# Loads and scores of an attention front end put into another order: third tile's q before the first regroupings, second tile's scores before the first mixing, k and v pieces spread over the double steps

## The chip, the cores and the metric

The program runs on one core of one Trainium2 chip. The metric is the device time of one execution in microseconds (us), as the median of several runs.

## The reference

Attention over 4 batches of 12 heads, 448 positions and 64 dimensions, whose heads are mixed by a 12 by 12 matrix before the softmax and by another one after it. Its output goes through an MLP-mixer block (a token MLP and a channel MLP, each with a residual).

```python
scores = (1 / np.sqrt(64)) * np.matmul(q, k.transpose(0, 1, 3, 2))
scores = np.einsum('bhij,hg->bgij', scores, w_pre)
scores = scores - np.max(scores, axis=-1, keepdims=True)
attn = np.exp(scores)
attn = attn / (np.sum(attn, axis=-1, keepdims=True) + 1e-09)
attn = np.einsum('bhij,hg->bgij', attn, w_post)
x = np.matmul(attn, v)                      # then (B, S, 768)
h = np.maximum(x.transpose(0, 2, 1) @ w_tok1, 0.0) @ w_tok2
u = x + h.transpose(0, 2, 1)
out = u + np.maximum(u @ w_ch1, 0.0) @ w_ch2
```

## The kernel before

**Tiles and groups.** The 448 query rows of a batch are four tiles `T` of 120, 120, 120 and 88 rows (`IT`), 16 tiles in all. `qk` computes the scores of one pair of heads of a tile on TensorE (8 matmuls in the trace) and copies them from PSUM into the tile `s` in SBUF, on ScalarE or, with `dve=True`, on VectorE. To mix heads by a matmul, the 12 heads of a query row must lie on partitions, so `regroup` (line 164) moves every 12th row of `s`, with all its heads, into a tile `r`: a DMA of 120 rows of 448 floats, SBUF to SBUF, on the queue of SyncE (SP). There are eight `r` tiles, so a regrouping is issued some eight groups ahead of its use. Two groups make a step.

**A step.** `pre` mixes the heads on TensorE (line 172, waits for two `r` tiles), `mx` takes the row maximum on VectorE, `ex` the exponential on ScalarE, `rec` the reciprocal on VectorE and the multiplication on GpSimd (POOL), `post` the second mixing on TensorE (line 214), `turn` transposes on VectorE. When a tile is complete, `av` multiplies by `v` in three pieces, and `store` writes the result `x` to DRAM.

**The order.** The main loop runs over double steps `J` from -2 on, two steps each, and the order of the calls in it is written out. Three tables say what a double step gets beside its steps: `score[J]` the `qk` calls for later tiles, `value[J]` the `av` calls, `loads[J]` the DMAs that bring q, k and v from DRAM. `loads[J + 1]` is issued at the end of double step `J`, behind that step's four regroupings. All these DMAs, regroupings, loads and stores alike, stand in one queue on SP, in program order; only a few of the first loads are issued by ScalarE. SP issues a DMA when its own waits are over, and each one waits too for the landing of the eighth DMA before it.

**Ahead of the loop** stand the loads of the first q and k, q of the second tile and a quarter of v, nine warm-up matmuls, the `qk` calls of tile 0, the first eight regroupings, and four of the six `qk` calls of tile 1; the other two stand in double steps -2 and -1.

**Behind the loop** come the transposes of `x` and the two MLPs, with weights that are split into two parts while TensorE works.

Of the kernel before, what the change touches and what calls it, by code (L numbers as in the profile page):

```python
# [19 lines left out]
B, H, S, D = 4, 12, 448, 64  # L20
DM = H * D
DT, DC = 256, 1536
JT = 4
IT = [(0, 120), (120, 120), (240, 120), (360, 88)]
GR = 10
HP = H // 2
# [10 lines left out]
def attn_mixer_kernel(  # L37
# [12 lines left out]
    nc = tc.nc  # L50
# [34 lines left out]
    AT, V = {}, {}  # L85
# [15 lines left out]
    NT = len(first)  # L101
# [9 lines left out]
    def load_q(T, h, m, eng):  # L111
        b, t = divmod(T, 4)
        i0, n = IT[t]
        if T not in Q:
            Q[T] = early.tile([128, HP, 120], F32, tag="q", bufs=3, name="q")
            if n < QP[t]:
                nc.gpsimd.memset(Q[T][:, :, n:QP[t]], 0.0)
        for s in range(2):
            o = H * i0 + (HP * s + h) * n
            eng[s].dma_start(  # L120
                out=Q[T][64 * s:64 * s + 64, h:h + m, :n],
                in_=q[b, :, o:o + m * n].rearrange("p (h i) -> p h i", h=m),
            )

    def load_v(b, part):
        if b not in V:
            V[b] = late.tile([128, H, JT, D], F32, tag="v", bufs=2, name="v")
        hs = slice(3 * part, 3 * part + 3)
        if part < 2:
            nc.sync.dma_start(out=V[b][:, hs], in_=v[b, :, hs])  # L130
            return
        lower, upper = slice(0, 64), slice(64, 128)
        nc.sync.dma_start(out=V[b][upper, hs, :3], in_=v[b, lower, hs, :3])
        nc.sync.dma_start(out=V[b][lower, hs, :3], in_=v[b, upper, hs, :3])
        nc.sync.dma_start(out=V[b][upper, hs, 3], in_=v[b, upper, hs, 3])

    def pair(tag, name):
        return (ps if tag == "pre" else ps_w).tile([128, 2, 512], F32, tag=tag, bufs=2, name=name)

    def qk(T, h, home="w", dve=False):  # L140
        b, t = divmod(T, 4)
        n = IT[t][1]
        if T not in S_t:
            S_t[T] = early.tile([120, H, S], F32, tag="s", name="s")
        p = pair(home, "qk")
        for c in (0, 64):
            m = min(64, QP[t] - c)
            for s in range(2):
                r = slice(64 * s, 64 * s + 64)
                nc.tensor.matmul(  # L150
                    out=p[c:c + m, s, :S], lhsT=Q[T][r, h, c:c + m], rhs=K[b][r, h, :], start=True, stop=True
                )
        if dve:
            nc.vector.tensor_copy(out=S_t[T][:n, h::HP, :], in_=p[:n, :, :S])
        else:
            nc.scalar.copy(out=S_t[T][:n, h::HP, :], in_=p[:n, :, :S])  # L156
# [111 lines left out]
    one = (nc.sync, nc.sync)  # L268
# [13 lines left out]
    for r in rt:  # L282
        nc.gpsimd.memset(r[:4], 0.0)
    load_q(1, 0, HP, one)
    load_v(0, 0)
    wz = et[0][:, 0].bitcast(BF16)
    nc.vector.memset(et[0], 0.0)
    for i in range(WARM):
# [4 lines left out]
    for x in range(2):  # L293
        ps_ = slice(64 * x, 64 * x + 64)
        nc.vector.tensor_tensor(
            out=kpre[ps_, :60].rearrange("p (i g) -> p i g", i=5),
# [5 lines left out]
    for s in range(2):  # L302
        ps_ = slice(64 * s, 64 * s + 64)
        for hf in range(2):
            nc.gpsimd.tensor_tensor(
                out=kpost[ps_, 32 * hf:32 * hf + 30].rearrange("p (g i) -> p g i", g=6),
# [165 lines left out]
    sf = [f // 2 for f in first]  # L472
    sl = [(f - 1) // 2 for f in first[1:]]
    loads = {J: [] for J in range(-2, ND)}
    score = {J: [] for J in range(-2, ND)}
    value = {J: [] for J in range(-2, ND)}
    for T in range(NT - 1):
        J = (sl[T] + 1) // 2
        n = sf[T + 2] // 2 - J
        if sf[T + 2] % 2 and sf[T + 2] // 2 > (sf[NT - 1] - 8) // 2:  # L480
            n += 1
        n = min(3, n)
        for hp in range(3):
            value[J + min(hp, n - 1)].append((T, hp))
    for h in range(HP):
        if h < 4:
            qk(1, h, ("pre", "w")[h % 2], h % 2 == 0)
        else:
            score[h - 6].append((1, h))
    for T in range(2, NT):  # L490
        hi = (sf[T] - 8) // 2
        lo = max((sl[T - 2] - 8) // 2 + 1 + (T == 4), hi - 2)
# [7 lines left out]
    uses = {}  # L500
    for J in range(-2, ND):
        score[J].sort()
        for T, h in score[J]:
            uses.setdefault((T, h), J)
    for T in range(2, NT):
        loads[max(-2, uses[T, 0] - 2)].append((load_q, T, 0, HP, one))
    for J, part in ((-1, 2), (0, 1), (2, 3)):
        loads[J].append((load_v, 0, part))
    for b in range(1, B):
        for h in range(0, HP, 2):  # L510
            J = uses[4 * b, 0] - 5 + h // 2
            loads[uses[4 * b, h] - 2 if b == 1 else J].append((load_k, b, h, 2, one))
        for part in range(JT):
            loads[sf[4 * b + 1] // 2 - 6 + part].append((load_v, b, part))

    def step(i):
        return steps[i] if 0 <= i < NS else []
# [284 lines left out]
```

## Time and profile before

| | |
|---|---|
| Median of 3 runs | 749.4 us (748.48 to 750.58) |
| Profiled execution, its own time | 757.26 us |
| Its span, from first to last instruction | 755.5 us |
| TensorE busy in the span | 735.6 us (97%) |
| VectorE, ScalarE, GpSimd busy | 410.7, 328.4, 303.7 us |
| Attention part, mixing steps | about 16 to 316 us |
| DMA: bytes, mean rate | 105.27 MB, 139 GB/s |
| TensorE clock granted | 1.0 in all slices |

The profiled execution is one run of the program with the profiler on; its 1.8 us outside of the span lie ahead of the first and behind the last instruction. An engine counts as busy while an instruction of it runs, matmuls by modelled ends. Idle time of an engine that nobody waits for costs nothing.

### The profile page before, as it was taken

The page shows a single profiled execution, that of the slowest core. Times are in us where ns is not written, and L with a number is a line of the kernel's source. Part 1 is how long each engine was busy: PE and PEld are TensorE (multiplying, and loading weights), DVE is VectorE, ACT ScalarE, POOL GpSimd, SP SyncE. Part 2 cuts the span into 40 slices and gives each one's busy share as a digit, 9 for nine tenths or more (in the row PEclk, how much of TensorE's full clock was granted, in tenths as well). Part 3 has the DMA queues.
Part 4 walks back from the last instruction along what each step waited for, and adds up shares of the span by engine and source line. Part 5 has one row for each costly group of instructions (what it writes and reads, how often), then busy time and mean ns, then how long its engine had stood idle before and what let it go on. Part 6 is the DMA issues. An engine that isn't in the chain of part 4 may idle for free. (4 is left out here: it accounts for less than half of the span.)

```text
span 755.5 us, 21850 instructions
## 1 busy us (share of the span) xinstructions
PE 735.6 (97%) x9209; PEld 570.5 (76%) x9209; DVE 410.7 (54%) x746; ACT 328.4 (43%) x732; POOL 303.7 (40%) x253
## 2 busy tenths in 40 slices
PE   8898999999999999899999999999999999999997
PEld 3354565556556555589988999999999999999997
DVE  3775676666766877778999999520004000220002
ACT  3776766776777777455544444300002000200000
POOL 3564665566656677757778777000000000000000
PEclk9999999999999999999999999999999999999999
DMA  6787667567756644735757655340003000020002
GB/s 180 240 232 213 199 194 229 190 192 217 231 175 228 217 165 159 265 104 198 252 178 221 169 170 162 147 146 1 1 1 146 1 1 1 0 74 1 0 1 74
DMA packets 66754, 105.27 MB, mean 139 GB/s; under 512 B 22835, under 2 KB 54624, under 8 KB 66144
## 3 DMA queue, kind: packets, MB, share of 16 engines
q1 hardware_dynamic: 66080, 102.96, 42.9%
q8 instruction: 73, 1.20, 0.7%
q10 hardware_dynamic: 480, 0.87, 0.5%
q14 instruction: 25, 0.20, 0.1%
q0 software_dynamic: 96, 0.03, 0.0%
HBM read 48.79 MB, written 16.52 MB: 86 GB/s over the span
## 5 line engine op out<-in xcount | busy, mean ns | idle before, releaser
L203 POOL TENSOR_TENSOR e<-e,sm 128x896 f32<-128x896 f32 x90 | 149.5, 1680 | 71.1 <-ACT e L189 25.9
L629 DVE SCALAR_TENSOR_TENSOR rl<-pc,rh 128x448 fp32r<-128x448 f32 x48 | 29.8, 621 | 218.7 <-ACT rh L628 218.7
L229 DVE STREAM_TRANSPOSE at<-post 128x896 f32<-128x896 f32 (+1 forms) x98 | 99.6, 1026 | 74.5 <-PE post L214 74.4
L628 ACT ACTIVATE rh<-pc 128x448 fp32r<-128x448 f32 x48 | 26.0, 542 | 232.9 <-PE pc L634 232.9
L189 ACT ACTIVATE e<-pre,sm 128x448 f32<-128x448 f32 x180 | 113.0, 640 | 5.5 <-DVE sm L198 4.8
L156 ACT COPY s<-qk 120x896 f32<-120x896 f32 (+1 forms) x91 | 81.6, 906 | 74.2 <-PE qk L150 70.5
L632 PE MATMUL pc<-u,w 128*128 128x448 f32 x288 | 105.3, 366 | 0.9 <-DVE u L665 0.9
L634 PE MATMUL pc<-u,w 128*128 128x448 f32 x288 | 105.2, 365 | 0.0
L633 PE MATMUL pc<-u,w 128*128 128x448 f32 x288 | 105.2, 365 | 0.0
L633 PE MATMUL po<-rl,w 128*128 128x448 f32 x288 | 105.2, 365 | 0.0
L634 PE MATMUL po<-rh,w 128*128 128x448 f32 x288 | 105.2, 365 | 0.0
L632 PE MATMUL po<-rh,w 128*128 128x448 f32 x288 | 105.2, 365 | 0.0
L180 DVE TENSOR_REDUCE sm<-pre 128x2 f32<-128x896 f32 x90 | 94.7, 1076 | 12.2 <-PE pre L172 12.1
L172 PE MATMUL pre<-r,kpre 64*64 64x448 f32 (+1 forms) x720 | 90.1, 550 | 4.0 <-DMA r<-s 2.7
L150 PE MATMUL qk<-k,q 64*64 64x448 f32 (+2 forms) x768 | 91.3, 542 | 2.7 <-issue 1.3
L246 PEld LDWEIGHTS av<-at,v 64*64 64x64 f32 x2688 | 73.8, 132 | 21.5 <-ACT s L156 10.4
L214 PE MATMUL post<-e,kpost 64*32 64x256 f32 (+1 forms) x2880 | 86.8, 355 | 3.1 <-issue 2.8
L422 POOL TENSOR_SCALAR cv_g<-cv_g 128x384 f32<-128x384 f32 (+1 forms) x52 | 82.3, 1585 | 18.2 <-ACT cv_g L416 18.2
L246 PE MATMUL av<-at,v 64*64 64x120 f32 (+1 forms) x2688 | 78.1, 259 | 3.0 <-issue 2.5
L214 PEld LDWEIGHTS post<-e,kpost 64*32 64x32 f32 x2880 | 51.0, 106 | 31.8 <-issue 21.5
L150 PEld LDWEIGHTS qk<-k,q 64*64 64x64 f32 (+2 forms) x768 | 28.8, 128 | 48.2 <-issue 20.5
L632 PEld LDWEIGHTS pc<-u,w 128*128 128x128 f32 x288 | 54.1, 188 | 5.5 <-DVE u L665 1.2
(78 smaller groups left out, 941.8 us busy)
## 6 DMA issues: line engine op xcount, KB each, us to landing
r<-s SPq DMA_DIRECT2D x172, 210.0 KB
cv_r<-in_w_ch_dram SPq DMA_DIRECT2D x48, 384.0 KB
xr<-x_dr SPq DMA_DIRECT2D x8, 672.0 KB
u_dr<-u SPq DMA_DIRECT2D x24, 224.0 KB
ur<-u_dr SPq DMA_DIRECT2D x4, 1344.0 KB
out_dram<-ur SPq DMA_DIRECT2D x24, 224.0 KB
k<-in_k_dram SPq DMA_DIRECT2D x20, 224.0 KB
x_dr<-x SPq DMA_DIRECT2D x36, 120.0 KB
```

Of the source, the lines that this page charges most:

```text
L150: nc.tensor.matmul(out=p[c:c + m, s, :S], lhsT=Q[T][r, h, c:c + m], rhs=K[b][r, h, :], start=True, stop=True)
L172: nc.tensor.matmul(out=p[64 * s:64 * s + 64, x, :S], lhsT=kpre[k], rhs=rt[a % NR][k], start=True, stop=True)
L180: nc.vector.tensor_reduce(out=s[:m, 0:2], in_=PP[st[0]][:m, :, :S], axis=AX.X, op=ALU.max, negate=True)
L189: nc.scalar.activation(out=E[st[0]][:m, x, :], in_=p[:m, x, :S], func=ACTF.Exp, bias=s[:m, x:x + 1], scale=1.0, accum_out=s[:m, 2 + 2 * x: ...
L203: nc.gpsimd.tensor_tensor(out=e[:m], in0=e[:m], in1=w.to_broadcast([m, 2, S]), op=ALU.mult)
L214: nc.tensor.matmul(out=p[32 * a:32 * a + 32, s, :S].rearrange("p (x f) -> p x f", x=2)[:, :, o:o + 32 * m], lhsT=kpost[k, 32 * hf:32 * hf ...
L229: nc.vector.transpose(out=AT[T][:, c:c + s1 - s0, :], in_=p[:, s0:s1, :S],)
L246: nc.tensor.matmul(out=p[64 * s:64 * s + 64, r, 10 * w * u:10 * w * (u + 1)], lhsT=V[b][k, 6 * u + h, j, :], rhs=at_[k, :w, :, f:f + 5], s ...
L422: nc.gpsimd.tensor_scalar(out=g[:P], in0=g[:P], scalar1=MAG_MIN, scalar2=MAG_MAX, op0=ALU.max, op1=ALU.min,)
L632: nc.tensor.matmul(out=p, lhsT=a[0], rhs=x[0], start=first, stop=False)
L633: nc.tensor.matmul(out=p, lhsT=a[0], rhs=x[1], start=False, stop=False)
L634: nc.tensor.matmul(out=p, lhsT=a[1], rhs=x[0], start=False, stop=last)
```

## The change

The loads of q for the third tile (T = 2) are issued ahead of the first regroupings, where the first quarter of v (`load_v(0, 0)`) stood; that quarter goes into the loop. All six `qk` calls of tile 1 stand ahead of the loop; the fifth is copied by VectorE, the sixth by ScalarE. `load_v` moves the two later quarters (parts 2 and 3) in two DMAs of 64 partitions instead of three: the fourth block of rows, of which one half is used, now comes for both halves. The parts of v come in the order 0, 2, 1, 3. For the second batch k comes in double steps 3, 4 and 5, one piece each; for later batches `place` puts k and v pieces each into the next double step that has no load yet.

```diff
--- before.py
+++ after.py
@@ -130,9 +130,8 @@
             nc.sync.dma_start(out=V[b][:, hs], in_=v[b, :, hs])
             return
         lower, upper = slice(0, 64), slice(64, 128)
-        nc.sync.dma_start(out=V[b][upper, hs, :3], in_=v[b, lower, hs, :3])
-        nc.sync.dma_start(out=V[b][lower, hs, :3], in_=v[b, upper, hs, :3])
-        nc.sync.dma_start(out=V[b][upper, hs, 3], in_=v[b, upper, hs, 3])
+        nc.sync.dma_start(out=V[b][upper, hs], in_=v[b, lower, hs])
+        nc.sync.dma_start(out=V[b][lower, hs], in_=v[b, upper, hs])
 
     def pair(tag, name):
         return (ps if tag == "pre" else ps_w).tile([128, 2, 512], F32, tag=tag, bufs=2, name=name)
@@ -282,7 +281,7 @@
     for r in rt:
         nc.gpsimd.memset(r[:4], 0.0)
     load_q(1, 0, HP, one)
-    load_v(0, 0)
+    load_q(2, 0, HP, one)
     wz = et[0][:, 0].bitcast(BF16)
     nc.vector.memset(et[0], 0.0)
     for i in range(WARM):
@@ -483,10 +482,7 @@
         for hp in range(3):
             value[J + min(hp, n - 1)].append((T, hp))
     for h in range(HP):
-        if h < 4:
-            qk(1, h, ("pre", "w")[h % 2], h % 2 == 0)
-        else:
-            score[h - 6].append((1, h))
+        qk(1, h, ("pre", "w")[h % 2], h % 2 == 0)
     for T in range(2, NT):
         hi = (sf[T] - 8) // 2
         lo = max((sl[T - 2] - 8) // 2 + 1 + (T == 4), hi - 2)
@@ -502,16 +498,28 @@
         score[J].sort()
         for T, h in score[J]:
             uses.setdefault((T, h), J)
-    for T in range(2, NT):
-        loads[max(-2, uses[T, 0] - 2)].append((load_q, T, 0, HP, one))
-    for J, part in ((-1, 2), (0, 1), (2, 3)):
-        loads[J].append((load_v, 0, part))
-    for b in range(1, B):
-        for h in range(0, HP, 2):
-            J = uses[4 * b, 0] - 5 + h // 2
-            loads[uses[4 * b, h] - 2 if b == 1 else J].append((load_k, b, h, 2, one))
-        for part in range(JT):
-            loads[sf[4 * b + 1] // 2 - 6 + part].append((load_v, b, part))
+    for T in range(3, NT):
+        loads[uses[T, 0] - 2].append((load_q, T, 0, HP, one))
+
+    def place(J, pieces):
+        for a in pieces:
+            while loads[J]:
+                J += 1
+            loads[J].append(a)
+
+    for b in range(B):
+        heads = [(load_k, b, h, 2, one) for h in range(0, HP, 2)]
+        parts = [(load_v, b, part) for part in (0, 2, 1, 3)]
+        if b == 0:
+            for J, a in zip((-1, 0, 1, 2), parts):
+                loads[J].append(a)
+        else:
+            if b == 1:
+                for J, a in zip((3, 4, 5), heads):
+                    loads[J].append(a)
+            else:
+                place(uses[4 * b, 0] - 4, heads)
+            place(sf[4 * b + 1] // 2 - 7, parts)
 
     def step(i):
         return steps[i] if 0 <= i < NS else []
```

**SP, start of the program.** First the queue of SP before, from the second tile's q on (`q`, `k`, `v` are loads from DRAM, `r` the regroupings):

```order
L120 DMA q<-in_q_dram 64x720 x2
L130 DMA v<-in_v_dram 128x768
L164 DMA r_93<-s 120x1x448
L164 DMA r_94<-s 120x1x448
L164 DMA r_95<-s 120x1x448
L164 DMA r_96<-s 120x1x448
L164 DMA r_97<-s 120x1x448
L164 DMA r_98<-s 120x1x448
L164 DMA r_99<-s 120x1x448
L164 DMA r_100<-s 120x1x448
L120 DMA q<-in_q_dram 64x720 x2
L164 DMA r_93<-s 120x1x448
```

Then the same place of the changed kernel:

```order
L120 DMA q<-in_q_dram 64x720 x4
L163 DMA r_93<-s 120x1x448
L163 DMA r_94<-s 120x1x448
L163 DMA r_95<-s 120x1x448
L163 DMA r_96<-s 120x1x448
L163 DMA r_97<-s 120x1x448
L163 DMA r_98<-s 120x1x448
L163 DMA r_99<-s 120x1x448
L163 DMA r_100<-s 120x1x448
L163 DMA r_93<-s 120x1x448
L163 DMA r_94<-s 120x1x448
```

The quarter of v ahead of the first eight regroupings is gone, two q loads stand in its place, and none stand between the eighth and the ninth regrouping.

**SP, double steps 2 to 4.** Before, the loads of the second batch's k (`x_dr<-x` are stores):

```order
L164 DMA r_100<-s 120x1x448
L120 DMA q<-in_q_dram 64x720 x2
L109 DMA k<-in_k_dram 64x896 x4
L265 DMA x_dr_59<-x 256x1x120
L164 DMA r_93<-s 120x1x448
L164 DMA r_94<-s 120x1x448
L164 DMA r_95<-s 120x1x448
L164 DMA r_96<-s 120x1x448
L109 DMA k<-in_k_dram 64x896 x2
```

The changed kernel, up to the store of the same double step; four regroupings and the third k pair follow on these rows as they do before:

```order
L163 DMA r_96<-s 120x1x448
L109 DMA k<-in_k_dram 64x896 x2
L163 DMA r_97<-s 120x1x448
L163 DMA r_98<-s 120x1x448
L163 DMA r_99<-s 120x1x448
L163 DMA r_100<-s 120x1x448
L120 DMA q<-in_q_dram 64x720 x2
L109 DMA k<-in_k_dram 64x896 x2
L264 DMA x_dr_59<-x 256x1x120
```

One pair of the four k loads has moved four regroupings ahead, out of the double step that also loads q.

**TensorE, first mixing.** Before, from the end of the fourth `qk` call of tile 1 on:

```order
L150 MATMUL qk<-k,q 56x448 x2
L172 MATMUL pre<-r_93,kpre 64x448
L172 MATMUL pre<-r_94,kpre 64x448
L172 MATMUL pre<-r_93,kpre 64x448
L172 MATMUL pre<-r_94,kpre 64x448
L150 MATMUL qk<-k,q 64x448 x2
L150 MATMUL qk<-k,q 56x448 x2
L172 MATMUL pre<-r_95,kpre 64x448
```

And of the changed kernel:

```order
L149 MATMUL qk<-k,q 56x448 x2
L149 MATMUL qk<-k,q 64x448 x2
L149 MATMUL qk<-k,q 56x448 x2
L149 MATMUL qk<-k,q 64x448 x2
L149 MATMUL qk<-k,q 56x448 x2
L171 MATMUL pre<-r_93,kpre 64x448
L171 MATMUL pre<-r_94,kpre 64x448
L171 MATMUL pre<-r_93,kpre 64x448
L171 MATMUL pre<-r_94,kpre 64x448
L171 MATMUL pre<-r_95,kpre 64x448
```

The two `qk` calls that stood between mixings stand ahead of the first one.

## Rows read from the trace of the kernel before

**Rows 1.** The page: busy time, and the group of the row maximum.

```profile
PE 735.6 (97%) x9209; PEld 570.5 (76%) x9209; DVE 410.7 (54%) x746; ACT 328.4 (43%) x732; POOL 303.7 (40%) x253
...
L180 DVE TENSOR_REDUCE sm<-pre 128x2 f32<-128x896 f32 x90 | 94.7, 1076 | 12.2 <-PE pre L172 12.1
```

**Rows 2.** Waits of PE over the span: us in total, times, longest.

```profile
PE post L214 <- issue: 2.8, 2, 1.8
PE pre L172 <- DMA r<-s: 2.7, 3, 1.8
...
PE qk L150 <- issue: 1.3, 1, 1.3
```

**Rows 3.** Timeline of PE, 60 to 124 us: start, duration, work, [idle before].

```profile
64.09 1.68 PE L150 MATMUL qk<-k,q 64*64 64x448 f32 x15
67.08 0.53 PE L150 MATMUL qk<-k,q 64*56 64x448 f32 x1 [1.32 <-issue]
...
74.13 0.65 PE L214 MATMUL post<-e,kpost 64*32 64x192 f32 x11 [1.79 <-issue]
...
122.78 0.62 PE L214 MATMUL post<-e,kpost 64*32 64x256 f32 x2 [0.98 <-issue]
```

**Rows 4.** Windows between the ends of these waits: engine busy (x records).

```profile
67.07:74.12 7.05, 5.25 (x126) 3.76 (x126) 2.21 (x2) 4.85 (x11) 2.13 (x2) 1.00 0.76 221
74.12:122.77 48.65, 47.67 (x1137) 28.13 (x1136) 32.18 (x60) 34.76 (x79) 28.77 (x24) 1.00 0.66 204
```

**Rows 5.** DMA queues, 60.3 to 64.3 us, then 64.3 to 64.5: packets, MB, share.

```profile
q1 hardware_dynamic: 510, 0.83, 92.7%
...
q8 instruction: 1, 0.02, 39.2%
```

**Rows 6.** Windows: PE, PEld, DVE, ACT, POOL busy, PEclk, DMA share, GB/s.

```profile
42.00:50.00 8.00, 8.00 (x218) 5.00 (x216) 5.88 (x10) 6.63 (x17) 4.88 (x4) 1.00 0.75 229
50.00:58.00 8.00, 8.00 (x185) 4.41 (x172) 5.98 (x12) 5.93 (x15) 4.36 (x5) 1.00 0.95 244
58.00:66.00 8.00, 7.76 (x167) 4.14 (x160) 5.91 (x12) 5.07 (x12) 4.52 (x4) 1.00 0.82 200
...
15.50:20.50 5.00, 4.27 (x30) 1.08 (x24) 2.17 (x2) 2.01 (x4) 0.00 (x0) 1.00 0.65 245
```

**Rows 7.** Timeline of SP, 44 to 124 us: start, duration, DMAs issued.

```profile
49.98 1.17 SPq L120 DMA_DIRECT2D q<-in_q_dram  x2
51.21 2.70 SPq L109 DMA_DIRECT2D k<-in_k_dram  x4
...
58.76 1.28 SPq L109 DMA_DIRECT2D k<-in_k_dram  x2
...
111.02 1.26 SPq L109 DMA_DIRECT2D k<-in_k_dram  x2
...
117.25 1.41 SPq L109 DMA_DIRECT2D k<-in_k_dram  x2
```

**Rows 8.** Timeline of SP, first 37 us.

```profile
7.82 0.58 SPq L130 DMA_DIRECT2D v<-in_v_dram  x1
13.82 6.89 SPq L164 DMA_DIRECT2D r<-s  x8
20.76 1.37 SPq L120 DMA_DIRECT2D q<-in_q_dram  x2
```

**Rows 9.** Timeline of PE, 12 to 33 us.

```profile
16.80 1.54 PE L172 MATMUL pre<-r,kpre 64*64 64x448 f32 x5 [0.62 <-DMA r<-s]
...
22.42 1.23 PE L172 MATMUL pre<-r,kpre 64*64 64x448 f32 x5 [1.80 <-DMA r<-s]
...
25.42 0.98 PE L172 MATMUL pre<-r,kpre 64*64 64x448 f32 x6 [0.25 <-DMA r<-s]
26.33 1.74 PE L214 MATMUL post<-e,kpost 64*32 64x256 f32 x64
```

**Rows 10.** Timeline of ACT, 12 to 31 us.

```profile
19.53 0.91 ACT L156 COPY s<-qk 120x896 f32<-120x896 f32 x1 [2.39 <-PE qk L150]
```

## The prediction

> **What bounds the kernel now.** I read the page first, then the waits of TensorE, then its timeline wherever such a wait is long, and last the queue of SP and the DMA shares at these places. TensorE is busy for 735.6 of 755.5 us, and no other engine comes near [rows 1]. The granted clock is 1.00 in every stretch read here [rows 4, 6], so a gain can only come out of TensorE's idle time, and what an order of loads can touch of it is little. The waits name two kinds [rows 2]. The first is `pre` waiting for a regrouping: 2.7 us in three pieces, all of them before the first `post` at 26.33 us [rows 2, 9]. The second is "issue", TensorE waiting for nothing that the profile can name.
>
> The second kind has a pattern. At 67.08 us TensorE goes on after 1.32 us with the last of 16 matmuls of two `qk` calls, 15 of which had run without a break; at 74.13 it stops for 1.79 us in the middle of a `post` and at 122.78 for 0.98 us, two matmuls before the end of one [rows 3]. Nothing in the code lies between those matmuls. From the first restart to the second there are 126 matmuls and 126 weight loads, 252 records, and from the second to the third 1137 and 1136, 2273 records, nine times that and a little more [rows 4]. So the stops sit on a fixed grid of the program: TensorE has run out of instructions, and the next block of about 256 is late. A DMA queue "instruction" carries one packet of 0.02 MB between 64.3 and 64.5 us, and none in the 4.0 us before, when the queue that carries all of SP's DMAs had a 92.7% share of the engines' time [rows 5]. I take it that the packet is late because the engine that moves it is full of loads.
>
> What fills them: SP issues q at 49.98 and four k DMAs at 51.21, behind them four regroupings and two more k DMAs at 58.76 [rows 7]. The DMA share is 0.75 from 42 to 50 us, 0.95 from 50 to 58, and 0.82 from 58 to 66 [rows 6]. With nothing but regroupings on the way, from 15.5 to 20.5 us, it is 0.65 at 245 GB/s [rows 6], so some of the engines are full while others rest, and a regrouping goes at that rate whatever the rest does.
>
> **The change part by part.** All sums are made against the profiled execution's 757.26 us (755.5 of span and 1.8 around it). It is 7.9 us longer than the median of 749.4; I carry the difference over to the median unchanged, which assumes that the waits are there without the profiler as well.
>
> *Start.* In place of a quarter of v, 128 x 768 floats or 384 KB, two q DMAs of 180 KB each go ahead of the first eight regroupings: 24 KB less, 0.1 us at 245 GB/s [rows 6]. SP issues v at 7.82 us and then waits until 13.82 for the scores, so neither the exchange nor the extra DMA delays the eight regroupings, which take 6.89 us to issue [rows 8]. The q DMAs at 20.76 (1.37 us [rows 8]) fall away behind them. But `pre` waits at 22.42 and 25.42 us for regroupings issued before those [rows 8, 9]; their order and time stay, so the 1.80 and 0.25 us stay. The two `qk` calls that move, 16 matmuls in about 1.8 us by 1.68 us for 15 [rows 3], fill the 0.62 us idle ahead of 16.80 [rows 9] and push the first `pre` by 1.2 us to 18.0. That costs nothing: it needs about 1 us (0.98 for six of its eight [rows 9]), the row maximum 1.08 [rows 1], so the exponential can start at 20.1; before, it stood behind the copy that ran from 19.53 to 20.44 [rows 10], which in the new order is earlier. If that cover were gone, the push of 1.2 us would be the price. Gain at the start: bounds -1.8 (the 22.42 wait goes) and +1.2; I take 0, as the wait's regroupings are untouched.
>
> *k of the second batch.* The double step with q and four k DMAs is the heavy one: four regroupings of 210 KB take 3.5 us at 244 GB/s [rows 6], q 1.5, four k DMAs of 224 KB 3.8, the store of 120 KB 0.5, in all 9.3 us, where double steps follow on each other in 6.2 (k at 111.02 and 117.25 [rows 7]). One k pair (1.9 us) moves ahead into the stretch from 42 to 50 us. That stretch has 8 x (0.95 - 0.75) = 1.6 us of unused share [rows 6], so the queue that TensorE's packets meet at 60 us is shorter by at most 1.6 us; at least by 0, if the engines that regroup were full all along. With 1.6 us the waits of 1.32 and 1.79 shrink to 0 and 0.19, a gain of 2.9; I take half of the shortening, 0.8 us, since the same early stretch gets other loads as well: 0.52 and 0.99 are left, a gain of 1.6.
>
> *k and v of the later batches.* `place` takes the k pair away from the q at 111.02 [rows 7]: 448 KB, 1.9 us less in that slot, where 0.98 us are lost at 122.78 [rows 3]. Bounds 0 and -1.0; I take -0.9, since the relief is twice the wait. The same happens twice more without a long wait behind it; I take 0.
>
> *v in two DMAs for three.* Two DMAs of 192 KB replace 144, 144 and 48 KB: 48 KB more, 0.2 us of engine time, and one issue on SP less (0.58 us for one of v [rows 8]). SP is not waited for, 0.
>
> *What gets crowded.* In double step 0 a quarter of v now shares the slot with a q: 3.5 + 1.1 (264 KB) + 1.6 = 6.2 us, within a shorter double step without `av`. Nothing waits there now; I take 0, bound +3.1, the two longest waits once more [rows 3].
>
> Sum: 0 - 1.6 - 0.9 = -2.5 us, 754.8 for the profiled execution and **746.9 us** for the median.
>
> **The rivals.** *The queue keeps its length.* By 60 us the same loads have been issued in either order; if the engines that carry regroupings never rest from 32 us on, the backlog is the same whatever came first, and only the third wait moves, by perhaps half: 749.4 - 0.4 = 749.0. For it: the 0.65 share with regroupings alone [rows 6]. Against it: the share does rise to 0.95, so the other engines had room.
>
> *The start shortens as well.* If the regroupings behind `pre` at 22.42 are late because of what lies ahead of them in the queue, less in front frees up to 1.8 us [rows 9] beside the 2.5: 745.1. Against it: v was issued six us ahead of the first of them [rows 8].
>
> *Slower: the crowded early slots.* With v and q together in double step 0 and k already in 2, the queue there may grow until a block of instructions comes too late twice, at 1.3 and 1.8 us as in rows 3: +3.1, 752.5. It decides as soon as the packet is some 3 us late, about half a double step. Against it: these double steps have no `av`, so TensorE uses up a block more slowly.
>
> *A packet does not queue.* By what TensorE shows, its packet might only take turns with SP's and be late for another cause; then no order of loads moves the waits: 749.4. The 92.7% share without an instruction packet [rows 5] speaks against turns. This is what the Trainium skill would have: its page "Runtime: NRT & Kernel Launch", section "Instruction fetch mechanics", has blocks of 16 KiB or 256 instructions, fetched while the one before runs, and calls the crossing "mostly hidden", and "DMA: Bandwidth & Descriptors", section "Queues, rings and completion order", lets an engine go round between queues packet by packet. The trace agrees with the 256; the three waits in rows 3 are not hidden. By these pages the sum would be 0.
>
> **How the numbers follow.** A measurement of this kernel can tell about 0.3%, 2.25 us, from no change. Chances: shorter waits as summed 0.44, of which 0.34 gain over 2.25 us and 0.10 less; a queue of the same length 0.24, no change; packets that do not queue 0.09, no change; the start too 0.12, faster; crowded slots 0.11, slower. Faster 0.46, same 0.43, slower 0.11. The time is that of the likeliest, 746.9; its own range is 745.0 to 748.6. The range for 8 in 10 reaches down to all three waits (4.1) with most of the start (1.7), 743.6, and up to one wait of 0.98 more than now, 750.4; left out are most of the slower case and a gain beyond the sum of all waits.
>
> **What the changed profile would show.** Right: the stops of TensorE at 67 and 74 us shorter by 0.8 us or more in sum, the one at 123 us gone, the first `post` within 0.5 us of 26.33, a DMA share from 42 to 50 us above 0.75 and from 50 to 58 below 0.95. Wrong: the same stops at the same matmuls with the same length (the queue keeps its length, or the packets do not queue); a new "issue" wait between 30 and 55 us (crowding); a first `post` that is more than a microsecond early or late (the start). The time itself would be wrong if the waits are an effect of the profiler, since then the median has nothing to lose there.

## The result and the profile after

The changed kernel takes 754.29 us (median of 17 executions, 751.94 to 761.67), the kernel before beside it on the same chip 751.10 (17 executions): ratio 1.0063, with an interval of 1.0035 to 1.0091. It is slower, by more than the 0.3% that a measurement can tell; 746.9 us was predicted, within 743.6 to 750.4. (Ratios here compare means without the executions more than 1.5% above a kernel's fastest, medians hold all; two of the kernel before are left out in this one, and with them the means are 755.65 and 752.01 us.)

The profiled execution of the changed kernel took 754.17 us, 752.4 of them span. Its page answers to [rows 1] with:

```profile
PE 732.8 (97%) x9209; PEld 569.7 (76%) x9209; DVE 412.3 (55%) x747; ACT 327.2 (43%) x731; POOL 303.8 (40%) x253
...
L179 DVE TENSOR_REDUCE sm<-pre 128x2 f32<-128x896 f32 x90 | 94.5, 1076 | 9.8 <-PE pre L171 9.8
```

The waits of TensorE, to be laid beside [rows 2] (us in total, times, longest):

```profile
PE pre L171 <- ACT e L188: 2.3, 5, 1.0
PE av L245 <- issue: 2.1, 2, 1.4
...
PE post L213 <- issue: 1.8, 1, 1.8
PE pre L171 <- issue: 1.2, 2, 0.7
...
PE pre L171 <- DMA r<-s: 1.1, 1, 1.1
```

And where they lie, in TensorE's timeline (start, duration, work, [idle before]), beside [rows 3, 9]:

```profile
18.73 3.44 PE L171 MATMUL pre<-r,kpre 64*64 64x448 f32 x16 [1.06 <-DMA r<-s]
23.20 1.10 PE L171 MATMUL pre<-r,kpre 64*64 64x448 f32 x8 [1.03 <-ACT e L188]
24.81 1.10 PE L171 MATMUL pre<-r,kpre 64*64 64x448 f32 x8 [0.50 <-issue]
...
66.53 0.98 PE L171 MATMUL pre<-r,kpre 64*64 64x448 f32 x8 [0.72 <-issue]
...
73.33 0.64 PE L213 MATMUL post<-e,kpost 64*32 64x192 f32 x10 [1.79 <-issue]
```

The stop near 67 us fell from 1.32 to 0.72, the one near 74 stayed at 1.79, the one at 122.78 is gone, and the pair of k that was moved is issued at 45.64 us, as the order says. The DMA shares went the way that the prediction asked for (columns as in [rows 6]):

```profile
42.00:50.00 8.00, 8.00 (x216) 5.18 (x200) 6.06 (x10) 6.51 (x17) 4.57 (x4) 1.00 0.83 214
50.00:58.00 8.00, 8.00 (x176) 4.49 (x172) 5.98 (x12) 5.67 (x15) 4.56 (x4) 1.00 0.90 216
58.00:66.00 8.00, 7.81 (x164) 4.45 (x156) 5.95 (x12) 5.08 (x12) 4.56 (x4) 1.00 0.80 211
```

But the kernel before, run once more (same1, below), has this from 50 to 58 us:

```profile
50.00:58.00 8.00, 8.00 (x188) 4.39 (x172) 5.95 (x12) 6.04 (x15) 4.33 (x5) 1.00 0.90 249
```

That is the lower share of 0.90 without any change. Of the two signs only the rise from 0.75 to 0.83 between 42 and 50 us, where same1 has 0.75 again, comes with the new order.

So one profile against the other says 3.1 us less, the direction that the prediction asked for, and the medians say 3.2 us more. The two can't both be typical. The execution of [rows 3] took 757.26 us, and of 191 executions of that kernel in all the sessions here ten took 755 or more.

### The profile page after: what moved, and what is told of

Its sections match the earlier page's. It is cut to its first block, busy times and chain, and to the rows that moved or that the text cites. A ratio compares the mean times of both kernels' runs of the same rounds, so it can differ in the third digit from the quotient of the medians.

```text
span 752.4 us, 21842 instructions
## 1 busy us (share of the span) xinstructions
PE 732.8 (97%) x9209; PEld 569.7 (76%) x9209; DVE 412.3 (55%) x747; ACT 327.2 (43%) x731; POOL 303.8 (40%) x253
## 5 line engine op out<-in xcount | busy, mean ns | idle before, releaser
L149 PE MATMUL qk<-k,q 64*64 64x448 f32 (+2 forms) x768 | 88.1, 541 | 2.3 <-DVE sm L197 1.2
L213 PE MATMUL post<-e,kpost 64*32 64x192 f32 (+1 forms) x2880 | 85.9, 355 | 2.3 <-issue 1.8
```

Of the source, the lines that this page charges most:

```text
L149: nc.tensor.matmul(out=p[c:c + m, s, :S], lhsT=Q[T][r, h, c:c + m], rhs=K[b][r, h, :], start=True, stop=True)
L213: nc.tensor.matmul(out=p[32 * a:32 * a + 32, s, :S].rearrange("p (x f) -> p x f", x=2)[:, :, o:o + 32 * m], lhsT=kpost[k, 32 * hf:32 * hf ...
```

## The experiments

All kernels ran in five rounds, twelve executions each, beside the kernel before on the same chip (23 to 35 executions each time, medians 750.67 to 751.36); not all rounds had the same chip.

### The kernel before once more, and three parts alone

**same1** is the kernel before, unchanged.

> The kernel before, unchanged, a second time: it shows how far two measurements of one program differ, and gives a second profile of it. If the profile before was an untypical one (757.26 us against a median of 751.1), this profile is shorter, near 751, and the stops of TensorE at 67, 74 and 123 us (1.32, 1.79, 0.98) are partly gone. If that profile was typical, the stops stand again and the profiled time is again some 6 us over the median. The ratio should be 1.000 within 0.003 either way.

Measured: 751.90 us, ratio 1.0008 (0.9988 to 1.0028). In TensorE's timeline of this profile (752.19 us):

```profile
17.01 1.55 PE L172 MATMUL pre<-r,kpre 64*64 64x448 f32 x5 [0.65 <-DMA r<-s]
...
66.48 0.53 PE L150 MATMUL qk<-k,q 64*56 64x448 f32 x1 [0.60 <-issue]
...
72.42 0.65 PE L214 MATMUL post<-e,kpost 64*32 64x192 f32 x11 [0.70 <-issue]
```

The same matmuls stop, at the same places of the program, but for 1.30 us in sum where [rows 3] have 3.11, and there is no stop at 122 us. Without any change of the loads 2.8 us of the waits that the prediction wanted to shorten are not there. The first profile was an unusually long execution.

**scores1**, only the two `qk` calls ahead of the loop:

```diff
-        if h < 4:
-            qk(1, h, ("pre", "w")[h % 2], h % 2 == 0)
-        else:
-            score[h - 6].append((1, h))
+        qk(1, h, ("pre", "w")[h % 2], h % 2 == 0)
```

> Only the two qk calls of tile 1 move ahead of the first mixing. If the start is what costs (first mixing pushed by up to 1.2 us, and the chain behind it with it), this alone is 1 to 2 us slower, 1.002, and the first post comes later than 26.3. If the loads are what costs, it is 1.000 and the first post stands where it stood.

**qfirst1**, only q first, and the first batch's v in the new slots:

```diff
-    load_v(0, 0)
+    load_q(2, 0, HP, one)
-    for T in range(2, NT):
+    for T in range(3, NT):
-    for J, part in ((-1, 2), (0, 1), (2, 3)):
+    for J, part in ((-1, 0), (0, 2), (1, 1), (2, 3)):
```

> Only the third tile's q goes ahead of the first regroupings, the first quarter of v into the loop, and the quarters of the first batch one double step each in the order 0, 2, 1, 3. If the crowded early slot (v and q together in double step 0) is what costs, this alone is 2 to 3 us slower (1.003 to 1.004) and its profile has a wait of TensorE inside a group between 60 and 75 us or a later first post. If the later loads cost, 1.000.

**spread1**, only the later k and v by `place`, k of the second batch in double steps 3, 4, 5, and v's later quarters in two DMAs (the added lines, without the definition of `place` and the edit of `load_v`, which are as in the change):

```diff
+            for J, a in zip((3, 4, 5), heads):
+                loads[J].append(a)
...
+            place(uses[4 * b, 0] - 4, heads)
+        place(sf[4 * b + 1] // 2 - 7, [(load_v, b, part) for part in (0, 2, 1, 3)])
```

> Only the later loads: k of the second batch in double steps 3, 4 and 5, k and v of the later batches one piece a double step, and the two later quarters of v in two DMAs. If the queue of loads around 60 us is longer because k comes earlier, this alone is 2 to 4 us slower (1.003 to 1.005), with waits inside a group at 66 and 72 us. If the spreading relieves the queue as the prediction had it, it is 1 to 3 us faster (0.996 to 0.999).

Measured: 750.80 (ratio 1.0008, 0.9992 to 1.0025), 750.58 (1.0003, 0.9982 to 1.0023) and 752.20 us (1.0026, 1.0004 to 1.0049). Neither part of the start costs or gains anything that these intervals can tell. The third part alone is slower by a little, so what it holds had to be taken apart.

### The whole change again, and the pairs

The edits are those above, two at a time: **qs1** q and scores, **qspread1** q and spread, **sspread1** scores and spread; **whole2** is all three, the changed kernel.

> The whole change again. If the loss of 0.6% is the change's own: 753 to 755 us, a ratio of 1.004 to 1.009. If it came from the chip or the hour: 750 to 752, as every part alone gave. In the profile, if late instruction blocks carry the loss: TensorE stops before 75 us by 1.5 us or more in sum, or a first post at 25.8 or later; in an execution near 750 neither.

> q first and the six scores first, later k and v as before. If the cost lies in k coming earlier or in what it adds to the crowded early slots: 749 to 751 us, ratio within 0.003 of 1. If q and the scores at the start are what is slow together: 753 to 755, with a first post at 25.8 or later.

> q first and the spread loads, scores as before. If the crowded early slots cost (a quarter of v beside a q, and k two double steps earlier, with nothing left between): 753 to 755 us, with stops of 1 to 2.4 us in double steps 5 to 7 of the profile. If the scores are needed for the loss: 750 to 752.

> Six scores first and the spread loads, q where it was. If q ahead of the regroupings is needed for the loss: about 752 us, what the spread loads alone gave (1.0026). If the moved scores shift the program's blocks of instructions against the loads so that more of them come late: 753 to 755.

Measured: whole2 754.28 us (1.0037, 1.0015 to 1.0059), qs1 751.17 (1.0019, 0.9988 to 1.0051), qspread1 751.82 (0.9995, 0.9976 to 1.0013), sspread1 754.76 (1.0047, 1.0020 to 1.0074). The loss is the change's own and comes back in another session. The scores and the spread loads make it together, q first isn't needed.

The trace of whole2, which took 758.42 us, shows where its time went. Below are windows of three stretches: from the end of the 10th to that of the 20th row maximum (about double steps 3 to 7), from the end of the last row maximum to the first `rl` of the channel MLP, and from there to the last `rl`. Left out is the stretch from the 20th to the last row maximum, 231.45 us in both. First the changed kernel's first profile, then whole2:

```profile
43.05:78.33 35.28, 32.78 (x704) 18.87 (x690) 22.83 (x41) 23.72 (x54) 18.77 (x14) 1.00 0.81 221
309.78:403.92 94.14, 89.40 (x869) 82.08 (x860) 80.50 (x143) 46.89 (x107) 64.83 (x56) 1.00 0.63 203
403.92:741.87 337.95, 337.95 (x1669) 313.25 (x1668) 113.40 (x210) 62.87 (x126) 50.05 (x31) 1.00 0.19 62
```

```profile
42.80:76.61 33.81, 32.66 (x704) 18.24 (x690) 22.83 (x40) 23.74 (x54) 18.79 (x14) 1.00 0.83 232
308.06:401.36 93.30, 89.30 (x869) 82.00 (x861) 80.29 (x143) 46.95 (x107) 65.12 (x56) 1.00 0.63 203
401.36:746.00 344.64, 344.64 (x1669) 313.00 (x1668) 113.71 (x210) 62.84 (x126) 49.89 (x31) 1.00 0.19 60
```

In the last row the same 1669 matmuls, TensorE busy throughout and its granted clock 1.00 in both, take 344.64 us where the first profile has 337.95, 6.7 us more: 206.5 against 202.5 ns each. The change has no instruction there. So two profiles of one and the same kernel differ most by a stretch that has none of the moved loads. In the other traces of this study its length is 337.9 or 344.6, nothing between; `before` and same1 have the short one.

### Which of the spread loads

**k1back**, the whole change with one k pair back where it was; **early1**, the kernel before with only that pair earlier; **late1**, the kernel before with only the later loads spread and k of the second batch as before; **three1**, the whole change with v in three DMAs:

```diff
k1back:
-                for J, a in zip((3, 4, 5), heads):
+                for J, a in zip((4, 4, 5), heads):
early1:
-            loads[uses[4 * b, h] - 2 if b == 1 else J].append((load_k, b, h, 2, one))
+            loads[3 + h // 2 if b == 1 else J].append((load_k, b, h, 2, one))
late1 (spread1 with):
-            for J, a in zip((3, 4, 5), heads):
+            for J, a in zip((4, 4, 5), heads):
and load_v as in the kernel before
three1:
-        nc.sync.dma_start(out=V[b][upper, hs], in_=v[b, lower, hs])
-        nc.sync.dma_start(out=V[b][lower, hs], in_=v[b, upper, hs])
+        nc.sync.dma_start(out=V[b][upper, hs, :3], in_=v[b, lower, hs, :3])
+        nc.sync.dma_start(out=V[b][lower, hs, :3], in_=v[b, upper, hs, :3])
+        nc.sync.dma_start(out=V[b][upper, hs, 3], in_=v[b, upper, hs, 3])
```

> The whole change, but the first k pair of the second batch back in double step 4 beside the q, where it was before. If that pair, moved a double step ahead, is what fills the queue before 75 us: 750 to 751.5 us, the stops of double steps 3 to 7 together under 1 us, and the 2 us that the later loads save kept. If the start or the later loads carry the loss: 753 to 755 as the whole change.

> Before, with only that one k pair a double step earlier. If the pair alone costs: 752 to 753 us, 1.002 to 1.003, with stops between 40 and 75 us in the profile that the kernel before hasn't. If it needs the q and the scores of the start as well: 750.5 to 751.5.

> Before, with only the k of batches 3 and 4 and the v of batches 2 to 4 spread, v in three DMAs as before. If the later loads save what they did in every profile so far (232.6 to 232.8 us from double step 8 to the last, against 233.3 to 235.5 without): 748.5 to 749.5, ratio 0.997 to 0.998. If that was chance: 750.5 to 751.5.

> The whole change, but v's later quarters in three DMAs as before. If the 48 KB more for each such quarter, or the two larger DMAs, carry the loss: 750 to 752 us. If not: 753 to 755, and the stretch from double step 8 on at 232.6 to 232.8 us as with two.

Measured: k1back 753.73 us (1.0055, 1.0026 to 1.0084), early1 750.51 (0.9995, 0.9976 to 1.0014), late1 750.34 (0.9983, 0.9964 to 1.0003), three1 752.56 (1.0017, 0.9995 to 1.0039). My theory of the k pair falls: alone it costs nothing, and put back it saves nothing that shows. So do the 2 us that I thought the later loads save: I had read them from counts of `post` records, of which some traces miss a few; late1 shows 0.8 us, within its interval. three1 lies between the change and the kernel before, half a microsecond above the 750 to 752 that would have settled it. What remained was the one edit of the load lines that I had priced at nothing, v in two DMAs.

### v in two DMAs

**two1** is the kernel before with that edit alone (the reverse of three1's lines); **three2** is three1 again; **wfour1** is the whole change with the bytes of two DMAs in pieces as small as before; **qlate1** joins qfirst1 and late1.

```diff
wfour1:
-        nc.sync.dma_start(out=V[b][upper, hs], in_=v[b, lower, hs])
-        nc.sync.dma_start(out=V[b][lower, hs], in_=v[b, upper, hs])
+        for js in (slice(0, 3), 3):
+            nc.sync.dma_start(out=V[b][upper, hs, js], in_=v[b, lower, hs, js])
+            nc.sync.dma_start(out=V[b][lower, hs, js], in_=v[b, upper, hs, js])
```

> Before, with v's later quarters in two DMAs for three and nothing else. If this form alone carries the loss: 752.5 to 754 us, 1.002 to 1.004, and over 33.5 us from the 10th to the 20th row maximum. If it only costs together with the moved loads: 750.5 to 751.5.

> The whole change with those quarters in four DMAs: the same bytes as in two, in pieces of 768 and 256 bytes a head as before. If the bytes carry the loss: 753 to 755 us. If the larger pieces do: 750.5 to 752.5.

> The whole change with v in three DMAs, again. If the two DMAs carry more than half of the loss: 751 to 752.6 us, ratio under 1.002. If the 752.6 of the first time was chance: 753 to 755.

> q first, and the later k and v spread, with k of the second batch and the scores as before and v in three DMAs. If each part's small gain adds: 748.5 to 750 us, 0.997 to 0.999. If the order of loads tells nothing as long as v comes in three DMAs: 750.5 to 751.5.

Measured: two1 751.89 us (1.0007, 0.9975 to 1.0039), wfour1 752.77 (1.0025, 0.9998 to 1.0051), three2 750.44 (1.0016, 0.9988 to 1.0044), qlate1 749.58 (0.9978, 0.9960 to 0.9997). three1 and three2 together, 24 executions, have a median of 751.6; the whole change, 29 executions, 754.3. Giving back the third DMA takes 2.7 us away. By resampling of the executions the means differ by 2.8, from 1.2 to 4.4. The two forms ran in different rounds; taken each against the kernel before beside it, the difference is 2.5, from 0.5 to 4.3. Of the executions below 755 us those with three DMAs average 751.3, those of the whole change 753.4. Alone the edit does little: two1 stands 1.0 above its neighbour, within its interval, and its profile missed what I expected, 32.05 us between the 10th and 20th row maximum instead of over 33.5. wfour1 lies between, so bytes, size of pieces and number of DMAs are not told apart.

Last a twin pair on one chip, **qlate2**, which is qlate1 again, and **qltwo1**, the same with v in two DMAs (two1's lines):

> q first and the later loads spread, v in three DMAs, again. If the 749.6 holds: 749 to 750.3 us, ratio 0.996 to 0.9995, no or one execution at 755 or more. If it was chance: 750.5 to 751.5.

> The same with v's later quarters in two DMAs. If this form is a cause: 751 to 753 us, 1.5 us or more above its twin, with two or more executions of 12 at 755 or more. If it is not: within 0.7 us of its twin.

Measured: qlate2 751.04 us (1.0006, 0.9978 to 1.0034), qltwo1 752.17 (1.0008, 0.9990 to 1.0026). The twin is 1.1 us slower, less than expected and no more than such a comparison can tell. And qlate1's gain did not come back: no kernel here is shown to be faster than the one before.

In the profile of qlate1 TensorE has no stop of the "issue" kind at 60 to 75 us; its longest over the span, 1.9, is an `av`. In that of qltwo1 there is one of 1.3 between 40 and 80 us (first qlate1 over the span, then qltwo1 from 40 to 80):

```profile
PE av L246 <- issue: 2.6, 2, 1.9
...
PE av L245 <- issue: 1.3, 1, 1.3
```

## Why the prediction was wrong

It missed by 7.4 us, in three parts of which each has its own step: 1.7 us in the base, 2.5 of gain that did not come, and 3.2 of loss that had no term.

**"I carry the difference over to the median unchanged, which assumes that the waits are there without the profiler as well."** This step failed, though not by the profiler: the profiled executions of all other kernels are among those that their medians are taken from. It failed because executions of one kernel differ by as much as the sum argues about. The base of 749.4 came from three executions; with 17 and more the median is 751.1. And the waits of [rows 3] come from an execution 6.2 us above that median: same1 has 1.30 us where they have 3.11, and lacks the third.

**Start, taken as 0.** Right in size: scores1, qfirst1 and qs1 lie within 0.2% of 1. The first `post` of the changed kernel begins at 25.84 us in its profile against 26.33 [rows 9], just within the half microsecond foretold. The reason given did not hold, so this is in part luck: the waits of 1.80 and 0.25 us for regroupings, which were to stay, are gone, and the first `pre` starts at 18.73 us instead of the 18.0 foretold, since TensorE waits 1.06 us there for a regrouping; behind it follow 1.03 us for the exponential and 0.50 of "issue".

**k of the second batch, -1.6.** No gain: early1, that pair alone, is at 0.9995, and with it put back the whole change stays at 753.73. The mechanism behind it, a packet of instructions queued behind loads, fits this trace as well, though no trace shows which engine the packet waited for. DMA queues of the changed kernel from 60 to 64 us, then from 64.0 to 65.1 (packets, MB, share):

```profile
q1 hardware_dynamic: 567, 0.90, 93.7%
...
q1 hardware_dynamic: 82, 0.19, 60.5%
q8 instruction: 1, 0.02, 5.9%
```

No instruction packet in 4 us at a 93.7% share, then one of 1.04 us (5.9% of 16 engines in 1.1 us), and TensorE goes on at 66.53, some 1.4 us behind its end. But "half of the shortening" was a guess about the execution of [rows 5], and the queue's length is not a constant of the kernel. "The queue keeps its length", 749.0, was the better rival for this term.

**k and v of the later batches, -0.9.** late1 gives -0.8 us, the forecast's size, but its interval includes 1, and same1 shows that the stop at 122 us can be absent without it. Open.

**v in two DMAs for three: "SP is not waited for, 0."** This is the term that was mis-sized: put at nothing, it is the largest of all. I had counted bytes (0.2 us of engine time) and issues, and looked for a wait on SP. Within the whole change the edit costs about 2.7 us of the 3.2; alone in the kernel before it shows as 1.0 us, undecided, and qltwo1 against its twin says 1.1.

**"What gets crowded", 0, with a bound of +3.1.** The rival "Slower: the crowded early slots" named 752.5 and the size was nearly right, but not the place: the quarter of v that shares a slot with a q is in qfirst1 and qs1 as well, and the earlier k in early1, and none of them is slower. Something like its sign, a block of instructions that is late at a new place, did come, though not in the changed kernel's own profile: k1back, sspread1, qspread1 and qltwo1 have "issue" stops at 53 to 62 us, where the kernel before has none.

**How the loss is made up.** The 29 executions of the whole change average 755.2 us, the 191 of the kernel before 751.4. Nine of the 29 took 755 or more, ten of the 191; those below 755 average 753.4 and 751.1. So 2.3 us are in the bulk of the executions, and the other 1.4 come from more of them at 755 or above. The edit of v accounts for most of the first part (below 755 us it is 753.4 against 751.3 with the third DMA given back).

The second part looks like the matmuls of the channel MLP at 206.5 ns: of the seven profiles that took 755 us or more six have them (whole2 758.42, qltwo1 758.84, three1 756.92, two1 755.37, wfour1 757.93 and qspread1 761.14), the kernel before's of 757.26 has not, and of the thirteen shorter ones none has. Over all kernels with two DMAs 28 of 101 executions took 755 or more, over the experiments' kernels with three 10 of 108; three1 shows that three DMAs do not exclude the slower spacing.

How the first part comes about is argued from profiles: the stretch of double steps 3 to 7 took 33.6 to 35.5 us in those of k1back, spread1, whole2, sspread1, qltwo1 and the changed kernel, 36.8 in qspread1's, and 31.6 to 33.1 in qfirst1, late1, qs1, scores1, both three and both qlate, with wfour1 at 33.3. But the kernel before itself has 35.8 and 33.9 there, early1 34.0 and two1 32.05, so the length of this stretch doesn't part the kernels cleanly, and with one profile for each it isn't shown. TensorE's "issue" waits between 40 and 80 us part them better: 0.6 to 2.5 us in sum in six of the eight profiles with two DMAs (not in spread1 and two1), none in the nine of the experiments' kernels that change the order and keep three, and none in wfour1. But the kernel before, with three DMAs, has them too, 3.1 us and 1.3 in same1, and the kernels without them are no faster than it. That late blocks are the way from the edit to the loss is likely by this, and not shown.

**What stays open.** Why two DMAs of 192 KB should delay more than three of 144, 144 and 48 when they hold 48 KB more, some 0.2 us; why the edit needs the moved scores to cost its full price; and what sets the spacing of the MLP's matmuls. One rival was not tested: as each DMA on SP waits for the landing of the eighth before it, two DMAs for three also change which landing every later one waits for, and no run keeps this apart from the shape of the load.

## What to carry to other kernels

When the stops that an edit is to remove are late instruction packets, they come and go from one execution to the next: take two or three profiles of the unchanged kernel before you price them, and a base from more than three executions. Price the edit that "is not waited for" too: in this kernel, whose DMA share is 0.80 to 0.90 between 42 and 66 us, the shape of a load mattered more than the slot in which it is issued. And when all parts together lose what no part alone loses, take parts away from the whole instead of adding them to the kernel before; k1back and three1 pointed in one step to what the single parts had not shown.

## What the runs showed of the hardware

- Matmuls of 448 columns that run without a break have two spacings at a granted clock of 1.00 (2.4 GHz): 202.5 and 206.5 ns on average over 1669 of them, 6.7 us in this kernel. In each profile one of the two holds from the start of the channel MLP to its end (start to start 202.7 or 206.7 ns in every 20 us of it); ahead of it the traces show no such difference.
- TensorE goes on some 1.4 to 1.6 us after the end of its instruction packet (66.53 against 65.08 us here; in the kernel before 67.08 against 65.65 and 74.13 against 72.54), so a packet that starts 4.0 us into a block (at 64.03 us) stops it, although the block lasts 6.5 us (from 60.00 us, 256 records of TensorE's instructions ahead of the stop, to 66.52). The Trainium skill, "Runtime: NRT & Kernel Launch", section "Instruction fetch mechanics", calls the crossing "mostly hidden"; here it is hidden in most blocks, and 0.72 us are not behind the 4 us in which the queue of loads took 93.7% of the engines' time.
- In three of the twenty profiles the granted clock fell to 0.50 (1.2 GHz) for 3.41 us in the middle of the span: at 309.09 us in scores1, 315.66 in qspread1 and 324.73 in sspread1. TensorE had just stopped: for 1.54 us until 309.11 in scores1, for 1.63 until 315.88 in qspread1, and three times, for 1.37, 1.29 and 0.62 us, between 311 and 324.4 in sspread1. It was at work while the clock was low, and the clock was back at 1.00 behind the 3.41 us. In sspread1 matmuls of 384 columns start 0.32 us apart at 0.50 and 0.17 behind it at 1.00. The profiles of the kernel before and of the change have no such fall, so it is no part of their difference.
